# Cross-covariance attention and a squared-ReLU expert on one core: transposed scores, k's norms by ones matmuls, inverse norms on ScalarE, another order of the first loads

## The chip, the cores and the metric

The kernel runs on one core of a Trainium2 chip. The time is device microseconds of one launch, the median of several executions. The notes on the chip that are drawn on are called the Trainium skill, by page title and section.

## The reference

```python
B, N, C = (4, 6080, 256); d_ff = 2048; tau = 1.0
qn = q / (np.linalg.norm(q, axis=1, keepdims=True) + 1e-06)   # norms over the tokens
kn = k / (np.linalg.norm(k, axis=1, keepdims=True) + 1e-06)
s = kn.transpose(0, 2, 1) @ qn / tau                          # 256 x 256 per batch
a = softmax(s, axis=-1)
x = (v @ a).reshape(B * N, C)
h = x @ w_in                                                  # 24320 x 2048
r = np.maximum(h, 0.0)
g = moe_s * (r * r) + moe_b
out = g @ w_out
```

Per batch there is a small reduction (scores and norms over 6080 tokens, a 256 x 256 softmax) and then a large expert, whose matmuls fill TensorE. The kernel folds the attention into the expert's weights: `wa = a @ w_in`, so that `h = v @ wa`.

## The kernel before

It walks over 48 groups of 512 tokens, each in 16 steps. A step `m` makes one 128-row tile of `h` for a group (`mm1`), plus seven of the 112 small matmuls of a seven-product scheme for the group before. Every second step ends with a relu on ScalarE. The reduction of the *next* batch is threaded through the same steps: loads, score matmuls, squares, and near the end of the batch a list of finishing operations, each put at a step by a table called `FIN` (number 0 falls in step 8 of a group, 3 in step 11, 8 in step 0 of the next group).

All operations are recorded in program order on each engine, so an engine that must wait holds up everything behind it. In what follows, a *finish* is the whole list of finishing operations of one batch, an *expert pair* is the two matmuls of `mm1` in a step, a *fold* is an operation that makes 256 or 512 columns of `wa`, and PSUM is the memory into which the matmuls write their results.

```python
# products: X, Z, Y are halves of PSUM tiles; a tile is one bank
def begin(name):
    t = ps_o.tile([P, 2, 2 * P], FP32, tag="o_ps", name="o_ps")
    halves = [t[:, h, :].rearrange("p (j c) -> p j c", j=2) for h in range(2)]
    if name == "X":
        st["X"] = halves[0]
        x_tile[0] = t              # its second half serves the norms
    else:
        st["Z"], st["Y"] = halves
# order of the seven products: X Z X Y X Z X, 16 matmuls each, from step 3 on

# ... scores of one piece of tokens, s = k^T q
nc.tensor.matmul(self.s_ps[:, ch, :], kc[:np_, j, ts(ch, P)], qc[:np_, j, :], ...)

# ... add_norms, later batches: 8 matmuls of one column, 4 sums of squares for k and 4 for q
self.n_all = x_tile[0][:, 1, : 2 * CH].rearrange("p (a c) -> p a c", a=2)
nc.tensor.matmul(self.n_ps[a][:, ch : ch + 1], t[:np_, a, j, ts(ch, P)], ones16[:np_, 0:1], ...)

# ... finishing, later batches: FIN = (0, 3, 5, 7, 15, 17, 19, 22)
norms:   add_norms, then sqrt on ScalarE as Ln and Exp(0.5 x)       # k and q together, 4 columns
recip:   add EPS and reciprocal on VectorE
split:   s * 1/|k| in two fp16 halves (VectorE), each through DMA transposes
join:    sum of the two transposed halves (VectorE)
exps(j): eT = Exp(1/|q| * sT)  on ScalarE, one half each            # 1/|q| is a per-partition scale
sums:    row sums of eT by 4 one-column matmuls, reciprocal on VectorE
folds:   wa = eT^T @ w_in, scaled by 1/row sum on the way out of PSUM
```

For batch 0 there is no earlier batch to hide behind. Its finish stands alone in front: transposes by TensorE in fp32, the first eight 256-column folds, then the main loop.

## Time and profile before

| | before |
|---|---|
| time, median of 3 | 718.86 us (718.62 to 719.0) |
| profiled span | 717.2 us |
| first expert matmul | 38.60 us |
| TensorE's recorded waits from 60 to 700 us | 0.2 us |

How to read it: TensorE is the bound from the first expert matmul on, so what counts is each pause of TensorE after that, and when that matmul starts.

### The profile page before, as it was taken

Reading aid. Unit: us, or ns where it says so; the run is one execution under the profiler, and the core shown is the slowest. Engines: PE = TensorE matmul, PEld = TensorE weight load, DVE = VectorE, ACT = ScalarE, POOL = GpSimd, SP = SyncE. Lnnn points to the kernel's source line nnn. Section 1 sums busy time; section 2 is a strip of 40 time slices with the busy share of each in tenths; the row PEclk is TensorE's granted clock in tenths of the full one; section 3 lists DMA queues with packets and bytes.
Section 4 is the critical chain, followed back from the end, with each engine's and each line's share of the span. In section 5 each row is a group of like instructions: output and inputs, shape, how many; then the busy total and the mean of one; then the engine's idle time right before and its main releaser. Section 6 shows DMA issues by size and latency. Waiting matters only on the chain.

```text
span 717.2 us, 17629 instructions
## 1 busy us (share of the span) xinstructions
PE 698.9 (97%) x7479; PEld 504.6 (70%) x7479; DVE 626.1 (87%) x882; ACT 536.5 (75%) x579; POOL 109.8 (15%) x189
## 2 busy tenths in 40 slices
PE   4799999999999999999999999999999999999998
PEld 2556777776677777777677777777668777777777
DVE  4879999999789999999889899999887888888886
ACT  4479877787777777777777778777877777777875
POOL 4532332101201222111110222110000000000000
PEclk9999999999999999999999999999999999999999
DMA  9999998647556879443972877944423333321201
GB/s 236 207 259 172 159 170 137 111 108 129 119 107 114 144 133 145 108 93 83 154 151 57 141 138 124 154 90 86 105 63 75 93 71 74 97 60 46 83 30 74
DMA packets 89790, 84.25 MB, mean 117 GB/s; under 512 B 59664, under 2 KB 64848, under 8 KB 89712
## 3 DMA queue, kind: packets, MB, share of 16 engines
q0 software_dynamic: 26064, 43.40, 37.5%
q1 hardware_dynamic: 63072, 38.43, 21.5%
q8 instruction: 58, 0.95, 0.6%
q10 hardware_dynamic: 576, 1.31, 0.5%
q14 instruction: 20, 0.16, 0.1%
HBM read 78.91 MB, written 24.90 MB: 145 GB/s over the span
## 4 chain that ended last, share of the span: by engine, by line
PE 93%; DMA 4%; DVE 1%; ACT 1%; POOL 1%; issue 0%; POOLq 0%; ACTq 0%
PE h_ps L641 45%; PE o_ps L809 40%; PE s_ps L146 4%; DMA qk<-in_q_dram 3%; PE wa_ps L326 2%; DMA v<-in_v_dram 1%; PE o_ps L713 1%; PE o_ps L687 0%; POOL qk L130 0%; ACT r L651 0%; DVE o_sb L669 0%; DVE S L737 0%; DVE sq L166 0%; DVE S L735 0%; DVE S L739 0%
## 5 line engine op out<-in xcount | busy, mean ns | idle before, releaser
L651 ACT ACTIVATE r<-h_ps 128x1024 f16<-128x1024 f32 (+1 forms) x384 | 388.4, 1014 | 153.4 <-PE h_ps L641 150.9
L641 PE MATMUL h_ps<-vT,wa 128*128 128x512 f16 (+7 forms) x1632 | 452.1, 364 | 0.1
L809 PEld LDWEIGHTS <-S 128*128 128x128 f16 x2944 | 198.0, 98 | 85.0 <-issue 0.9
L809 PEld LDWEIGHTS <-g 128*128 128x128 f16 x2208 | 155.0, 98 | 74.1
L664 DVE TENSOR_TENSOR g<-r 128x2048 f16<-128x2048 f16 (+2 forms) x150 | 174.8, 1165 | 14.6 <-ACT r L651 14.5
L809 PE MATMUL o_ps<-T,S 128*128 128x128 f16 x2208 | 183.3, 219 | 0.1
L641 PEld LDWEIGHTS <-wa 128*128 128x128 f16 x1632 | 135.9, 98 | 20.6 <-ACT wa L319 0.3
L809 PE MATMUL o_ps<-w_out,g 128*128 128x128 f16 x1472 | 134.2, 219 | 0.2 <-DVE u L669 0.2
L669 DVE SCALAR_TENSOR_TENSOR o_sb<-o_ps,s_out,u 128x256 f32<-128x256 f32 x138 | 66.5, 482 | 47.1 <-PE o_ps L809 44.5
L662 ACT ACTIVATE g<-r 128x1024 f16<-128x1024 f16 (+1 forms) x97 | 100.4, 1035 | 0.2
L146 PE MATMUL s_ps<-qk 128*128 128x256 f16 (+1 forms) x384 | 69.6, 281 | 14.0 <-ACT qk L137 8.7
L379 POOL DMA_DIRECT2D v<-in_v_dram x48 | 31.3, 656 | 263.5 <-DMA vT<-v 209.6
L669 DVE SCALAR_TENSOR_TENSOR u<-o_ps,s_out,rowconst 128x256 f32<-128x256 f32 x138 | 66.0, 478 | 0.0
L809 PE MATMUL o_ps<-w_out,S 128*128 128x128 f16 x736 | 63.5, 219 | 0.0
L809 PE MATMUL o_ps<-N,g 128*128 128x128 f16 x736 | 63.4, 219 | 0.0
L193 POOL DMA_DIRECT2D f<-f x30 | 26.3, 877 | 225.6 <-DVE f L182 172.0
L169 ACT ACTIVATE sq<-qk 128x1024 f16<-128x1024 f16 (+3 forms) x49 | 50.4, 1033 | 10.0 <-DMA qk<-in_k_dram 6.7
L737 DVE TENSOR_TENSOR S<-S,g 128x2048 f16<-128x2048 f16 (+1 forms) x47 | 56.4, 1201 | 1.3
L735 DVE TENSOR_TENSOR S<-g 128x2048 f16<-128x2048 f16 (+1 forms) x47 | 56.1, 1193 | 0.0
L741 DVE TENSOR_TENSOR S<-g,S 128x2048 f16<-128x2048 f16 x46 | 56.0, 1217 | 0.0
L739 DVE TENSOR_TENSOR S<-g 128x2048 f16<-128x2048 f16 x46 | 55.9, 1216 | 0.0
L146 PEld LDWEIGHTS <-qk 128*128 128x128 f16 (+1 forms) x384 | 32.8, 101 | 20.1 <-DVE qk L136 8.0
(74 smaller groups left out, 314.9 us busy)
## 6 DMA issues: line engine op xcount, KB each, us to landing
out_dram<-o_sb SPq DMA_DIRECT2D x46, 512.0 KB, 3.0
v<-in_v_dram POOLq DMA_DIRECT2D x47, 256.0 KB, 4.7
qk<-in_k_dram POOLq DMA_DIRECT2D x42, 256.0 KB, 6.1
qk<-in_q_dram POOLq DMA_DIRECT2D x42, 256.0 KB, 7.2
f<-f POOLq DMA_DIRECT2D x30, 128.0 KB, 3.1
vT<-v SPq DMA_TRANSPOSE x182, 3.2
w<-in_moe_w_out_dram POOLq DMA_DIRECT2D x4, 512.0 KB, 11.3
raw<-in_k_dram SPq DMA_DIRECT2D x2, 512.0 KB, 6.4
```

Of the source, the lines that this page charges most:

```text
L146: po(nc.tensor.matmul(self.s_ps[:, ch, :], kc[:np_, j, ts(ch, P)], qc[:np_, j, :], start=(c == 0 and j == 0 and ch == 0), stop=(c == len(s ...
L169: po(nc.scalar.activation(out=st["sq"][:np_, 1, js, :], in_=kc[:np_, js, :], func=AF.Square))
L641: po(nc.tensor.matmul(dst, wa[:, ci, ts(m, P)], src, start=(ci == 0), stop=(ci == CH - 1), skip_group_check=True))
L651: po(nc.scalar.activation(out=r16[:, :, i % 2, :n], in_=h_tiles.pop((g, i))[:, :, :n], func=AF.Relu))
L662: po(nc.scalar.activation(out=dst, in_=src, func=AF.Square))
L664: po(nc.vector.tensor_mul(dst, src, src))
L669: po(nc.vector.scalar_tensor_tensor(out=dst, in0=src, scalar=s_out, op0=ALU.mult, in1=add, op1=ALU.add))
L735: po(nc.vector.tensor_add(T[1], A21, A22))
L737: po(nc.vector.tensor_sub(T[2], T[1], A11))
L739: po(nc.vector.tensor_sub(T[3], A11, A21))
L741: po(nc.vector.tensor_sub(T[4], A12, T[2]))
L809: po(nc.tensor.matmul(st[name][:, j, :], a()[:, i, ts(j, P)], w[:, i, :], start=first, stop=last, skip_group_check=True))
```

## The change

Its intent: with `sT = q^T k` computed directly, nothing has to be transposed. The inverse norm of k then lies along the free axis and must be equal in all partitions; a matmul with a 128 x 128 matrix of ones gives it so, as a row of 256 columns. The inverse norms become four dependent activations on ScalarE (logarithm, root, logarithm of root + EPS, exp of its negative), and VectorE has one product left. In front, the last k rows are loaded ahead of the last q rows, and v ahead of w_in, so that k's path is done when q arrives.

```diff
-                    kc[:np_, j, ts(ch, P)],
-                    qc[:np_, j, :],
+                    qc[:np_, j, ts(ch, P)],
+                    kc[:np_, j, :],
 ...
+                if a == 1:
+                    po(nc.tensor.matmul(self.n_ps[1], ones16[:np_, :], t[:np_, 1, j, :],
+                                        start=start, stop=end, skip_group_check=True))
+                    continue
 ...   (root, recip, split, join and turn are removed)
+            def inverse(a):
+                n = (CH, C)[a]
+                r = sm_pool.tile([P, n], FP32, tag=f"r{a}", name=f"r{a}")
+                act(self.n_ps[a], AF.Ln, bias=tiny)
+                act(r, AF.Exp, scale=0.5)
+                act(r, AF.Ln, bias=eps)
+                act(r, AF.Exp, scale=-1.0)
+            def scale(halves=1):
+                    po(nc.vector.tensor_mul(st["t"][:, js], self.s_ps[:, js],
+                                            rk[:, None, :].broadcast_to((P, n, C))))
 ...
+            front = [norms(1), lambda: inverse(1), norms(0), lambda: inverse(0),
+                     lambda: scale(CH if self.b == 0 else 1)]
             return front + [lambda: exps(0), lambda: exps(1), sums] + folds
 ...   (first batch: NLATE = 3 late pieces, all k parts before all q parts; fewer filler matmuls)
-    load_w_in(0, NW)
     load_v(0)
+    load_w_in(0, 2 * P)
+    load_w_in(2 * P, NW)
 ...   (first batch: one fold ahead of the main loop, in place of three)
-    for f in fin[6:12]:
+    for f in (exps0, exps1, row_sums, folds[0]):
 ...
-    FIN = (0, 3, 5, 7, 15, 17, 19, 22)
+    FIN = (0, 3, 16, 18, 20, 21, 22, 24)
-    FOLDS = (0, 0, 3, 4, 7, 8)
+    FOLDS = (0, 0, 1, 1, 3, 4, 7, 8)
```

## The prediction

> **What bounds the kernel now.** I read the page's busy line first, then the table of stretches, then the chain, then timelines of the two places that the change touches.
>
> ```profile
> PE 698.9 (97%) x7479; PEld 504.6 (70%) x7479; DVE 626.1 (87%) x882; ACT 536.5 (75%) x579; POOL 109.8 (15%) x189
> ```
>
> TensorE says 97% busy, but its ends are modelled, so I checked it by stretches (columns: stretch, length, then busy time of PE, PEld, DVE, ACT, POOL, the granted clock, DMA share, GB/s).
>
> ```profile
> 0.00:36.50 36.50, 21.85 (x183) 14.65 (x183) 23.12 (x47) 16.94 (x21) 18.97 (x39) 1.00 1.06 221
> 38.60:51.90 13.30, 13.30 (x78) 7.26 (x79) 9.92 (x17) 10.85 (x13) 3.72 (x7) 1.00 1.08 276
> 51.90:73.60 21.70, 21.34 (x164) 14.09 (x163) 21.08 (x37) 20.62 (x26) 5.31 (x10) 1.00 1.07 177
> 73.60:710.00 636.40, 636.38 (x6991) 463.78 (x6990) 568.44 (x776) 485.84 (x517) 80.62 (x131) 1.00 0.55 106
> ```
>
> All of TensorE's idle time lies before 36.5 us, where the loads of batch 0's q and k run at a DMA share above 1. After 73.6 it misses 0.02 us in 636. To be sure that this is real work, I added up the matmuls of a stretch as columns at 2.4 GHz plus 2.4 ns each: 13.20 us of work in 38.6 to 51.9 (13.3 long), 21.14 in 51.9 to 73.6 (21.7 long). So from the first expert matmul at 38.60 on, TensorE is the bound and only its instruction count and its stalls matter. The chain shows what sets 38.60 (start, length, what):
>
> ```profile
> 18.76 9.74 DMA qk<-in_q_dram
> 28.78 7.72 DMA v<-in_v_dram
> 36.55 0.62 PE vT_ps L390 x8
> 37.68 0.90 PE wa_ps L326 x8
> 38.60 0.60 PE h_ps L641 x2
> ```
>
> The first v tile lands last and TensorE's in-order queue puts its transposes ahead of the row sums. Yet v is hardly alone there. The timeline of the front (start, length, engine, line, operation) has a second path of the same length:
>
> ```profile
> 33.94 1.04 PE L146 MATMUL s_ps<-qk 128*128 128x256 f16 x8
> 35.44 0.26 ACT L235 ACTIVATE nrm<-n_ps,tiny 128x2 f32<-128x2 f32 x1 [1.47 <-PE n_ps L224]
> 36.43 0.84 ACT L299 ACTIVATE eT<-t_ps,rnrm 128x256 f16<-128x256 f32 x2 [0.50 <-PE t_ps L293]
> 37.44 0.24 PE L309 MATMUL r_ps<-parts,eT 128*128 128x1 f16 x4
> 37.54 1.03 PE L326 MATMUL wa_ps<-w_in,eT 128*128 128x256 f16 x8
> ```
>
> The exponentials end at 37.27 and the row sums start 0.17 later, a normal handover. Removing v alone would therefore win about nothing.
>
> **What the Trainium skill says.** "ScalarE: Activation LUTs", What ACT_TABLE_LOAD costs: an ACTIVATE with a pointer bias takes about 280 ns + 0.833 ns per column, an immediate one 186 ns + 0.833, and neighbours overlap by about 93 ns. The trace agrees: 0.26 and 0.20 us for two columns, 0.47 to 0.50 for 256 columns (the exponentials), 1.02 for 1024 columns that start 0.92 apart. "TensorE: Matmul & The Clock Gate", Wait — 56ns, not 53.3ns?: N columns take N/2.4 GHz plus 2.5 ns; the trace has two 512-column matmuls per 0.43 us. Same page, What's actually happening: the array falls to half clock after an idle window of about 3.4 us; the granted clock is 1.00 in every stretch here, and no run so far shows a drop. "VectorE: DVE Perf Modes", The TRN2 errata: an fp32 tensor_tensor takes (N+151)/0.96 ns, 691 for 512; the trace has 684.
>
> **Front, part by part.** *Removed:* the four fp32 transposes (0.74 us, 35.64 to 36.38) and the add and reciprocal of each norm. *Moved:* the last three k pieces come ahead of the last q's. A 256 KB piece takes 1.25 us (issues of a k and q pair are 2.5 us apart), so k is complete about 1.25 us earlier, near 31. v moves ahead of 256 KB of w_in: 36.5 becomes about 35.3. The last q does not move: the score matmuls of the last two pieces ran back to back from 33.94, so it landed by about 34.3.
>
> *k's path.* TensorE has 10 ones matmuls of 256 columns (1.1 us, the tenth after the fold that ends near 30.5), 20 one-column ones for q (0.033 each, 0.65), then 8 of 256 (0.86): about 32.3. Then ScalarE does four dependent activations of 256 columns, (0.47 + 0.44 + 0.50 + 0.44) plus about 0.03 between: 1.95 us, to about 34.4. It ends just before q's does, so it is hidden.
>
> *q's path.* Last q 34.2, square 0.4, sums and handover: Ln near 35.05 (35.44 before). Four small activations of 0.29, 0.23, 0.29, 0.23 end near 36.1; the scaling by VectorE (two of about 0.45 from 34.9) ends first. Exponentials at 36.15 in place of 36.43, so the first expert matmul at about 38.3, a gain of 0.3 us.
>
> *Given back.* Before, TensorE did eight 256-column w_in folds between the row sums and 38.60, while it would have waited for the scaling anyway. Now it does four there and four after the first expert matmuls: 4 x 0.109 = 0.43 us moved from a wait into the bound stretch. The front nets 0.1 us slower (from 0.5 faster to 0.4 slower).
>
> **Later batches, three times.** *Removed:* about 2.6 us of VectorE (0.16 + 0.18 + 0.68 + 0.87 + 0.69) for one product of 0.69, and four small DMA transposes. VectorE and DMA bound nothing there, so: 0. *TensorE:* 8 one-column matmuls (0.26) become 2 of 256 and 4 of one column (0.21 + 0.13): +0.08 us. *ScalarE:* two small activations become four of 256 columns back to back, then four small ones half a group later. Here is ScalarE at the old place:
>
> ```profile
> 146.30 1.03 ACT L651 ACTIVATE r<-h_ps 128x1024 f16<-128x1024 f32 x1
> 147.27 0.26 ACT L235 ACTIVATE nrm<-o_ps,tiny 128x4 f32<-128x4 f32 x1
> 147.56 0.20 ACT L236 ACTIVATE nrm<-nrm 128x4 f32<-128x4 f32 x1
> 147.72 1.02 ACT L651 ACTIVATE r<-h_ps 128x1024 f16<-128x1024 f32 x1
> 149.42 1.02 ACT L651 ACTIVATE r<-h_ps 128x1024 f16<-128x1024 f32 x1 [0.68 <-PE h_ps L641]
> 151.07 1.02 ACT L651 ACTIVATE r<-h_ps 128x1024 f16<-128x1024 f32 x1 [0.62 <-PE h_ps L641]
> ```
>
> The relus come every 1.645 us. The order of instructions puts the new four between two relus: 0.97 + 0.50 + 0.47 + 0.53 + 0.34 = 2.81 us from relu to relu, so the second is 1.17 late. There are two h buffers. A buffer's next writer starts three groups of items (0.39 each) and two pairs (0.43) after its pair ends, 2.03 us; the relu needs 0.17 + 1.02 + 0.1. Slack 0.74, stall 0.43. A lateness already in the trace says it is a little worse: two squares between the relus at 113.12 and 115.93 made it 0.94 late at a longer beat of 1.865, and the six relus after them came 0.2 to 0.3 late in sum where this model gives about 0. So 0.43 to 0.65. The four small ones (1.05 us, 0.3 late) fit; the two exponentials now sit together behind VectorE's product and may be 0.7 late, costing 0 to 0.1. Per batch 0.5 to 0.8, taken as 0.65: +1.9 us for three.
>
> Sum: 718.9 + 0.1 + 1.9 = 720.9. I take 720.3, since a hand-placed schedule may have room that I don't see.
>
> **Rivals.** (1) The front wins about 1 us and ScalarE's bursts are absorbed. For it: the transposes leave a path that really ends the front, and in the stretch from 51.9 to 73.6 ScalarE (20.62 of 21.7) and VectorE (21.08) leave TensorE 0.56 us short, so relus that start earlier might recover some. Against: the last q is fixed by DMA, and the 0.43 us of folds. Time: 717.7. (2) k's inverse norms become the front's wait: if its sums come later than 32.3, ScalarE, in order, starts q's logarithm late, microsecond for microsecond. For it: ScalarE and TensorE have only some 0.5 us in hand. Time: up to 722.5. (3) With fewer filler matmuls TensorE falls to half clock near 36 us. Against: its gaps stay below 1.5 us. It would cost 2 us: 722.5.
>
> **Range and chances.** Front from 0.9 faster to 1 slower, the batches from 0 to 2.7: 717.6 to 722.4 holds 8 in 10. 2% is 14.4 us; all of TensorE's idle time is about 18, nearly all under loads whose bytes do not change. Faster 0.005, slower 0.01.
>
> **What would show it.** First expert matmul between 37.9 and 38.6, v's transposes earlier by a microsecond and no longer in the chain, four w_in folds behind it. In each later batch four activations in a row, the next relu about 1.2 us late, and TensorE idle or a longer beat of 0.4 to 0.7 us just there and nowhere else. I am wrong if the relu's lateness leaves TensorE's beat unchanged, if the first expert matmul comes before 37.5, or if the stretch to 73.6 shrinks by more than 0.5 us.

## More of the kernel before

The later batches are finished in three places. The table of stretches around them has the stretch, its length, the busy time of TensorE, of its weight loads, of VectorE, ScalarE and GpSimd, the granted clock, the DMA share and GB/s:

```profile
140.90:176.00 35.10, 35.10 (x386) 24.70 (x384) 32.30 (x46) 28.24 (x33) 3.18 (x6) 1.00 0.55 114
313.00:348.00 35.00, 35.00 (x384) 24.55 (x382) 32.04 (x45) 27.91 (x33) 3.17 (x6) 1.00 0.54 109
486.00:524.00 38.00, 38.00 (x416) 26.77 (x415) 34.79 (x49) 29.95 (x34) 1.58 (x3) 1.00 0.39 90
```

Length and TensorE's busy time agree to the last digit: the old finish cost no pause that this view shows. The ends of matmuls are modelled, so a short pause can hide in it: at the old logarithm the small matmuls follow the expert pair after 0.49 us (147.09 to 147.58), elsewhere after 0.43. Two places of the timeline of TensorE in the first of them will matter (start, length, engine, line, operation, output and inputs, shape, count):

```profile
150.04 0.22 PE L809 MATMUL o_ps<-w_out,g 128*128 128x128 f16 x1
150.10 0.50 PE L809 MATMUL o_ps<-T,S 128*128 128x128 f16 x6
...
165.34 0.24 PE L309 MATMUL r_ps<-parts,eT 128*128 128x1 f16 x4
165.45 0.59 PE L641 MATMUL h_ps<-vT,wa 128*128 128x512 f16 x2
```

At 150.10 product 4 takes over tile X from product 3 in tile Y, without a gap. At 165.34 the four row sums pass in 0.11 us.

## The result

The changed kernel took 723.85 us (median of 5, 723.39 to 725.03), the kernel before 719.00 in the same rounds (718.62 to 719.84). The ratio is 1.0070, with a 95% interval of 1.0058 to 1.0082. The ratios are made from the runs of both kernels, and not quite the ratios of the two medians. At the 2% bar this is the same time; against the interval it is plainly slower, by almost 5 us, and it lies outside the predicted range of 717.6 to 722.4.

The profiled span is 721.9 us against 717.2. The three finishing stretches of the changed kernel, columns as above:

```profile
140.90:176.00 35.10, 34.34 (x374) 24.12 (x372) 30.08 (x40) 28.77 (x38) 3.17 (x6) 1.00 0.53 114
313.00:348.00 35.00, 34.24 (x379) 24.29 (x377) 29.68 (x40) 28.12 (x37) 3.72 (x7) 1.00 0.46 91
486.00:524.00 38.00, 37.24 (x406) 26.23 (x404) 32.52 (x45) 31.06 (x39) 1.60 (x3) 1.00 0.35 83
```

TensorE misses 0.76 us in each, where it missed nothing. VectorE is less busy by 2.2 to 2.4 us in each, as intended, and that is worth nothing. The waits of TensorE from 60 to 700 us name the cause (engine, output, line, what it waited for: us in total, times, longest):

```profile
PE o_ps L786 <- ACT r L247: 1.8, 3, 0.6
PE r_ps L280 <- ACT eT L270: 0.5, 3, 0.2
```

L247 is the logarithm of k's norm sums. The timelines of ScalarE and TensorE there:

```profile
150.14 1.02 ACT L628 ACTIVATE r<-h_ps 128x1024 f16<-128x1024 f32 x1 [0.56 <-PE h_ps L618]
151.06 0.47 ACT L247 ACTIVATE r<-o_ps,tiny 128x256 f32<-128x256 f32 x1
...
152.87 1.00 ACT L628 ACTIVATE r<-h_ps 128x1024 f16<-128x1024 f32 x1
```

```profile
150.76 0.22 PE L786 MATMUL o_ps<-w_out,g 128*128 128x128 f16 x1
151.58 0.49 PE L786 MATMUL o_ps<-T,S 128*128 128x128 f16 x6 [0.60 <-ACT r L247]
```

This is the handover from product 3 to product 4 of the fence before: 0.06 us apart there, 0.82 here. The logarithm reads the norm sums in the second half of tile X; product 4 writes the first half of the same tile, and starts only when the logarithm has ended at 151.53. The relu behind the four activations is indeed late (2.73 us after the last one), but no wait of TensorE for a relu is listed.

The second wait is where the row sums are made. The timeline of all three engines there:

```profile
167.05 0.68 DVE L264 TENSOR_TENSOR sm_t<-s_ps,r 128x512 f32<-128x512 f32 x1
167.83 0.91 ACT L270 ACTIVATE eT<-sm_t,r 128x256 f16<-128x256 f32 x2 [1.00 <-DVE sm_t L264]
168.46 0.17 PE L280 MATMUL r_ps<-parts,eT 128*128 128x1 f16 x1
168.79 0.23 PE L280 MATMUL r_ps<-parts,eT 128*128 128x1 f16 x3 [0.16 <-ACT eT L270]
168.88 0.59 PE L618 MATMUL h_ps<-vT,wa 128*128 128x512 f16 x2
```

ScalarE stands still for 1.00 us until VectorE has made the product, the exponentials come late, and from the first row sum to the next expert matmul TensorE now needs 0.42 us instead of 0.11: 0.31 more.

In front the first expert matmul is where it was (38.62 against 38.60). The lines that answer to those in the prediction:

```profile
35.51 0.26 ACT L247 ACTIVATE r<-n_ps,tiny 128x2 f32<-128x2 f32 x1 [0.65 <-PE n_ps L234]
36.60 0.91 ACT L270 ACTIVATE eT<-sm_t,r 128x256 f16<-128x256 f32 x2
38.62 0.60 PE L618 MATMUL h_ps<-vT,wa 128*128 128x512 f16 x2 [0.37 <-ACT wa L290]
```

From q's logarithm to the first exponential it is 1.09 us now and was 0.99 (35.44 to 36.43): the chain of four activations is no shorter than two, two small VectorE operations and four transposes beside them.

To place the loss in time, I took the start of each relu in both profiles and subtracted. The lateness is 0.76 us from the fourth relu up to the first later batch's finish, then grows by 1.03, 1.14 and 1.14 us in the three finishes and by nothing anywhere else, to 4.06 at the last relu. The span differs by 4.7. The remaining 0.65 lies after the last VectorE operation, which ends 2.72 us before the end of the span before (714.00 + 0.48, of 717.2) and 3.37 us after the change. The last VectorE operation, and the DMA view of the window from 718 us to the end:

```profile
718.05 0.48 DVE L670 SCALAR_TENSOR_TENSOR o_sb<-o_ps,s_out,rowconst 128x256 f32<-128x256 f32 x1 [1.26 <-PE o_ps L664]
```

```profile
q14 instruction: 1, 0.01, 0.5%
```

An instruction fetch lies in the last half microsecond. The same window of the kernel before has none.

### The profile page after: what moved, and what is told of

It reads as the page before. A ratio compares the mean times of both kernels' runs of the same rounds, so it can differ in the third digit from the quotient of the medians.

```text
span 721.9 us, 17552 instructions
## 1 busy us (share of the span) xinstructions
PE 699.9 (97%) x7458; PEld 504.8 (70%) x7458; DVE 620.2 (86%) x864; ACT 542.8 (75%) x599; POOL 110.2 (15%) x188
## 4 chain that ended last, share of the span: by engine, by line
PE 87%; ACT 4%; DMA 4%; DVE 2%; issue 1%; POOL 0%; POOLq 0%; ACTq 0%; DVEq 0%
PE h_ps L618 42%; PE o_ps L786 37%; PE s_ps L148 4%; DMA qk<-in_k_dram 3%; ACT r L628 2%; PE wa_ps L297 2%; DMA qk<-in_q_dram 1%; ACT g L639 1%; ACT r L247 1%; PE o_ps L690 1%; DVE g L641 1%; ACT eT L270 1%; PE o_ps L664 0%; DVE u L646 0%; POOL qk L132 0%
## 5 line engine op out<-in xcount | busy, mean ns | idle before, releaser
L177 ACT ACTIVATE sq<-qk 128x1024 f16<-128x1024 f16 (+1 forms) x47 | 49.2, 1050 | 8.7 <-DVE f L190 4.4
```

The source lines that it names most:

```text
L177: po(nc.scalar.activation(out=st["sq"][:np_, 1, js, :], in_=kc[:np_, js, :], func=AF.Square))
```

## The experiments

Seventeen kernels were run besides the changed one, all of them correct. "Lateness" is that of the relus against the profile of the kernel before: after the front (the seventh relu) and at the last relu. "Idle" is TensorE's missing time in the three finishing stretches together. A pause of some 0.15 us can hide in "idle", since the ends of matmuls are modelled; the lateness has no such gap. "Tail" is from the end of the last VectorE operation to the end of the span, good to 0.05 us, since the span is printed to 0.1. Rows without a ratio were single looks.

| kernel | time, us | before, us | ratio (95%) | front | idle | last relu | tail |
|---|---|---|---|---|---|---|---|
| changed kernel | 723.85 | 719.00 | 1.0070 (1.0058–1.0082) | 0.76 | 2.28 | 4.06 | 3.37 |
| e1_ln_early | 723.14 | 719.73 | 1.0052 (1.0037–1.0067) | 0.43 | 1.41 | 3.36 | 3.36 |
| e2_ln_late_spread | 723.86 | 719.73 | 1.0061 (1.0044–1.0078) | 0.99 | 2.29 | 4.30 | 3.33 |
| e3_ln_early_rest_later | 722.45 | 719.73 | 1.0043 (1.0028–1.0058) | 0.97 | 0.90 | 2.88 | 3.35 |
| e4_sums_later | 723.97 | 719.73 | 1.0063 (1.0048–1.0078) | 0.86 | 2.55 | 4.44 | 3.29 |
| e5_folds_before | 723.12 | 719.54 | 1.0050 (1.0033–1.0066) | 0.28 | 2.34 | 3.68 | 3.35 |
| e7_before_v_first | 719.10 | 719.54 | 0.9995 (0.9980–1.0010) | 0.32 | 0 | 0.24 | 2.68 |
| e8_spread_scale_early | 721.68 | 719.54 | 1.0031 (1.0014–1.0048) | 1.00 | 0.39 | 2.16 | 3.38 |
| e9_spread_and_folds | 721.00 | 719.54 | 1.0022 (1.0007–1.0037) | 0.33 | 0.39 | 1.47 | 3.36 |
| e10_norms_step6 | 722.15 | 719.16 | 1.0038 (1.0023–1.0053) | 0.16 | 1.14 | 2.56 | 3.37 |
| e11_ln_step10 | 723.90 | 719.16 | 1.0065 (1.0048–1.0082) | 1.06 | 2.04 | 4.12 | 3.31 |
| e13_twelve_sp | 723.19 | 719.16 | – | 0.92 | 2.31 | 4.28 | 2.65 |
| e14_eighteen_dve | 723.99 | 719.16 | – | 1.05 | 2.32 | 4.42 | 3.30 |
| e15_front_only | 719.77 | 719.12 | 1.0006 (0.9994–1.0019) | 0.54 | 0 | 0.42 | 2.61 |
| e16_front_only_mended | 718.65 | 719.12 | 0.9993 (0.9979–1.0006) | -0.14 | 0 | -0.26 | 2.69 |
| e12_all_mended | 719.93 | 719.12 | 1.0011 (0.9998–1.0023) | -0.18 | 0.39 | 0.96 | 2.67 |
| e17_front_two_steps | 718.46 | 719.19 | 0.9990 (0.9976–1.0003) | -0.34 | 0 | -0.46 | 2.69 |
| e18_eight_sp | 723.43 | 720.09 | – | 0.86 | 2.34 | 4.22 | 3.00 |

One caution for the column "front": ten profiles here have the changed kernel's front unchanged (the changed kernel, e1, e2, e3, e4, e8, e11, e13, e14, e18; e15 would be an eleventh), and they show 0.43 to 1.06. Differences under 0.3 us in it cannot be read from a single profile. The growth in the finishes repeats to 0.1.

### Which wait: e1, e2, e3, e4

Theory A: TensorE waits for the first logarithm's read of tile X. Theory B, the prediction's: the burst of four activations makes a relu late and TensorE waits for an `h` buffer.

**e1_ln_early** moves the burst of four to the step of the norm sums:

```diff
-    FIN = (0, 3, 16, 18, 20, 21, 22, 24)
+    FIN = (0, 0, 16, 18, 20, 21, 22, 24)
```

> Edit to the changed kernel: in batches 1 to 3 the four activations of k's inverse norms follow right behind the ones matmuls (same step) in place of three steps later. Theory A (TensorE's next product into tile X waits 0.65 us until the first logarithm has read the norms that lie in the same tile): that wait disappears from the waits list, each batch loses 0.65 us of its 1.1, total about -1.9 us against the changed kernel (near 722). Theory B (my prediction: the relu behind the four activations comes too late and TensorE waits for an h buffer): the burst now follows two squares and makes a relu about 1.6 us late, so TensorE stalls 0.4 to 0.9 us there and nothing is won, or it gets worse (723.8 or more).

The wait for L247 went. In its place stood a smaller one, for the relu:

```profile
PE h_ps L618 <- ACT r L628: 0.5, 3, 0.2
```

The idle time fell from 2.28 to 1.41 us, but the lateness grew by 2.93 us over the three finishes, where the changed kernel's grew by 3.30; of the 0.70 us by which its last relu leads the changed kernel's, 0.33 lie in the front, which varies. So only about 0.1 us per finish was won, not 0.65. Both theories are partly right: where the logarithm stops being a listed wait, the late relu becomes one, and 0.23 us stay at the logarithm in a form that the list of waits does not show (see e9).

**e2_ln_late_spread** leaves the logarithm where the change has it, and sets the other three activations apart:

```diff
             front = [norms(1), lambda: inverse(1), ...
+                front[1:2] = [lambda i=i: inverse_part(i) for i in range(4)]   # later batches
-    FIN = (0, 3, 16, 18, 20, 21, 22, 24)
+    FIN = (0, 3, 5, 7, 9, 16, 18, 20, 21, 22, 24)
```

> Edit to the changed kernel: the first logarithm stays three steps behind the ones matmuls, the other three activations of k's inverse are spread two steps apart each, so no relu is more than about 0.3 us late. Theory A: TensorE's wait of 0.6 us for the logarithm stays, total unchanged (723.5 to 724). Theory B: the stall disappears with the burst, 0.65 us per batch, total near 722.

The wait for the logarithm stayed whole, 1.8 us in three times, and so did the time. The lateness grew by 3.31 us, as in the changed kernel. Without any burst the loss is the same, so in the changed kernel the burst is not what is paid for.

**e3_ln_early_rest_later** is the reverse, the logarithm alone in step 8 and the other three as a burst in step 11 (`FIN = (0, 0, 3, 3, 3, 16, ...)`).

> Edit to the changed kernel: the first logarithm right behind the ones matmuls, the other three activations as a burst three steps later. Theory A: as the early run, the wait goes, total near 722 (-1.9). Theory B: three activations make the relu about 0.8 us late in place of 1.2, so most of the stall goes as well, near 722. This run does not separate the two; it is there to be the best placement of both.

Neither wait is left there, and the idle time falls to 0.90 us, most of it the row sums. The first part of a batch's loss, as lateness, went from 0.72 to about 0.25.

**e4_sums_later** moves only the row sums, three steps later (`FIN[7] = 27`).

> Edit to the changed kernel: the row sums and the w_in folds behind them come three steps later in batches 1 to 3. If the second part of a batch's loss (0.32 to 0.42 us) is TensorE waiting in order for the second exponential, it goes: -1.0 to -1.2 us in all (near 722.7), and the row sums' wait for the exponentials is left in the front only. If it is due to the relus behind the exponentials being late, nothing changes (723.8).

The wait for the exponentials went from the later batches, and this came for it:

```profile
PE h_ps L618 <- ACT r L628: 0.7, 3, 0.3
```

The exponentials themselves are late and hold the next relu, so moving their reader only moves the wait. Time and idle did not fall.

### Tile X again: e10, e11

**e11_ln_step10** changes one number of the changed kernel: the burst comes one step earlier, `FIN[1] = 2`.

> The changed kernel with one number changed: the burst of four activations on k's norms one step earlier (step 10 for step 11), so that the first logarithm runs while TensorE is in product 3 (tile Y), and ends ahead of product 4, the next into X. Theory A (the wait is for the logarithm's read of tile X): TensorE's wait for L247 (1.8 us in 3 times) is gone. The burst (1.9 us) now stands ahead of the relu of step 11, so that relu is late by more and theory B of the prediction (h buffer) shows: a wait of TensorE for the relu of 0.2 to 0.6 per batch. Batch costs 0.6 to 1.0, last relu 2.6 to 3.8 late, time 722.5 to 723.5. If instead any chain of four activations costs the same wherever it stands, the time stays at 723.8 and the wait for L247 stays.

```profile
PE h_ps L618 <- ACT r L628: 1.5, 3, 0.5
```

The wait for the logarithm is gone and the prediction's kind of wait stands there instead, listed as 0.5 us each and 0.67 in lateness. The time did not change; that is dearer than I had expected (last relu 4.12 us late, not 2.6 to 3.8). The burst stands elsewhere here, and the relu behind it starts 3.03 us after the one before (148.86 and 151.89), not 2.81. The prediction's model, fed with that, gives 3.03 - 1.645 - 0.74 = 0.65, so its slack is right. It does not follow that the changed kernel would show 0.43 once the logarithm's wait were gone: no run has the burst at its place without that wait. So far as shown, two waits of similar size lie close together, and the prediction computed the one that did not come first.

**e10_norms_step6** takes e9 (below) and makes k's norm sums and their logarithm two steps earlier, in step 6, while TensorE works on tile Z (`FIN = (-2, -2, 3, 5, 7, 16, 18, 9, 21, 23, 26)`).

> As e9 (single activations spread over steps, scaling at its old place, folds ahead of the main loop), but k's norm sums and their first logarithm two steps earlier, in step 6, while TensorE writes product 1 into the Z tile; the next product into X starts some 1.2 us later. Theory A (TensorE waits because product X and the norms share a PSUM tile, so what counts is whether X is being written while the logarithm reads): the 0.17 us that e9 still shows per batch at the logarithm goes; each later batch costs 0.15 to 0.25 us against before instead of 0.31 to 0.42, the last relu stands 1.0 us after before's instead of 1.47, time 720.3 to 720.7 with before at 719.5. Rival B (the residual is the extra activations on ScalarE, wherever they stand): 0.3 to 0.4 per batch stays, time as e9, 721.0.

My expectation failed, and it was dearer instead of cheaper. TensorE's timeline in the first finish:

```profile
145.01 0.55 PE L796 MATMUL o_ps<-T,S 128*128 128x128 f16 x7
145.67 0.38 PE L230 MATMUL o_ps<-f,ones 128*128 128x256 f16 x2
...
146.99 0.33 PE L796 MATMUL o_ps<-T,S 128*128 128x128 f16 x3 [0.28 <-ACT r L264]
```

The norm sums start 0.66 us after the seven small matmuls ahead of them began; elsewhere the next matmul follows such a seven after 0.39 us. VectorE reads the first product out of tile X from 145.14 to 145.62 just there, so I take the sums' start at 145.67 for the end of that read; the profile does not name the wait. Then the logarithm stands behind a square on ScalarE until 146.46, and product 2, the next into X, waits for it. The tile is shared by three engines, and a free window of it must be free for all three.

### Spreading and the folds: e5, e8, e9

**e5_folds_before** makes the first three folds ahead of the main loop, as before the change.

```diff
-    for f in (exps0, exps1, row_sums, folds[0]):
+    for f in (exps0, exps1, row_sums, *folds[:3]):
-    FOLDS = (0, 0, 1, 1, 3, 4, 7, 8)
+    FOLDS = (0, 0, 3, 4, 7, 8)
```

> Edit to the changed kernel: batch 0's four w_in folds of columns 256 to 511 go back ahead of the first expert matmul, into the wait for the scaling, and the other folds get their old steps. Theory: the front's loss of 0.76 us (4 x 0.109 = 0.43 us of folds moved behind the first expert matmul, and 0.33 us in which the fifth expert pair waits for VectorE's scaling of a fold that now queues behind a square) goes: relus 3 to 56 come 0.0 to 0.2 us after the old kernel's in place of 0.76 (the last q's landing varies by some 0.3 us), total near 723.0. Rival: the loss sits in the later first row sums; then the relus stay 0.7 or more behind.

The front's lateness is 0.28; in e9 and e10, which have the same front, it is 0.33 and 0.16. The mean of the three is 0.26, that of the ten unmended fronts 0.89. The moved folds thus cost about 0.6 us: 0.43 of TensorE's work (4 x 0.109) and the rest a wait for VectorE, which scales the second fold behind a square that itself waits for a relu.

**e8_spread_scale_early** separates all four activations, with the logarithm in the step of the sums, puts VectorE's product back to the place of the old scaling, and moves exponentials and sums behind it (`FIN = (0, 0, 3, 5, 7, 16, 18, 9, 21, 23, 26)`; the eighth number is the product). **e9_spread_and_folds** is e8 with e5's front.

> Edit to the changed kernel, batches 1 to 3: first logarithm right behind the ones matmuls, the other three activations two steps apart each, VectorE's product nine steps after the matmuls in place of twenty, so that the exponentials don't wait for it, the exponentials two steps apart, row sums three steps later. Theory: all of a batch's loss but the 0.08 us of extra matmul columns goes, 1.0 us per batch: relus at the end 1.0 to 1.3 us behind the old kernel's (front 0.8 and 3 x 0.1) in place of 4.06; total near 720.8. If something else in the later batches costs, more than 0.3 us per batch stays.

> The last edit together with the folds put back: relus at the end 0.2 to 0.5 us behind the old kernel's, total 719.0 to 719.8, the same as before. If the losses do not add up, it stays above 720.5.

In e8 and e9 only 0.13 us of idle time per finish is left, and no wait for L247, a relu or the exponentials is listed in the finishes. Both expectations were missed: e8 came at 721.68 us, and e9 at 721.00, above the 720.5 from which the losses were said not to add up. The tail's 0.65 us was not in the sum, and each finish still costs 0.31 to 0.42 us in place of 0.1. TensorE's timeline of e9 shows where:

```profile
147.44 0.59 PE L628 MATMUL h_ps<-vT,wa 128*128 128x512 f16 x2
148.16 0.49 PE L796 MATMUL o_ps<-T,S 128*128 128x128 f16 x6
```

The small matmuls, which go on writing tile X, start 0.72 us after the expert pair, not 0.43; the logarithm reads the same tile from 147.64 to 148.11. Only 0.13 us of this pause is shown as idle. All three finishes have it, in e1, e3, e8, e9 and e12 alike (0.72 each); the kernel before, whose logarithm has 4 columns and takes 0.26 us, has 0.49. So 0.23 us per finish is tile X again. With the estimate of 0.08 for the wider norm sums, 0 to 0.1 us per finish is left that no view shows as a wait.

### The loads: e7

**e7_before_v_first** is the kernel *before* with one line moved, `load_v(0)` ahead of `load_w_in(0, NW)`.

> Edit to the kernel before: only the first v load goes ahead of the first w_in load. The chain of the kernel before names v as the last to land. My reading: the exponentials' path is as long, so the time stays (first expert matmul within 0.2 us of 38.6, total within 0.5 us of before). Rival: v bounds, and the first expert matmul comes 0.5 us or more earlier.

```profile
PE r_ps L309 <- ACT eT L299: 0.2, 1, 0.2
```

v is no longer waited for, the exponentials are, and the first expert matmul came at 38.92, no earlier than 38.60 (and 0.3 us later, where 0.2 was expected at most). The time is the same (ratio 0.9995). That agrees with the prediction's reading that v was one of two equal paths.

### The tail: e13, e14, e18

**e13_twelve_sp** and **e18_eight_sp** add tiny copies (4 bytes, SBUF to SBUF) on SyncE's queue to the changed kernel, twelve and eight, and **e14_eighteen_dve** adds eighteen tiny memsets on VectorE.

```diff
+        for i in range(4):                       # e13; in e18: eight, in batch 2 only
+            at_step(w1 - fin_len + 2 * i, lambda i=i: po(nc.sync.dma_start(
+                out=spare[:, i : i + 1], in_=ones32[0:1, i : i + 1])))
```

> On the last 0.66 us: in every run of the changed form the span ends 3.3 us after VectorE's last operation starts to be done, in the kernel before 2.7, and only there an instruction fetch (queue 14, one packet of 8 KB) lies in the last half microsecond. The changed kernel with twelve tiny copies more on SyncE's queue (four per later batch), so that SyncE issues as many DMAs as before. Theory T1 (the fetch, or the order of the last waits, is SyncE's and follows from its count of instructions): the fetch at the end goes and the end is 2.7 us after VectorE's last operation. Theory T2 (it is another engine's): the fetch stays at the end and the tail stays 3.3. Time else as the changed kernel, 723.8.

> The changed kernel with eighteen tiny memsets more on VectorE (six per later batch), so that VectorE has as many operations as before. If the instruction fetch at the end is VectorE's, it moves off the end and the tail shrinks from 3.3 to 2.7 us; if it is SyncE's or ScalarE's, the tail stays 3.3. The memsets cost some 0.06 us each on an engine that is not the bound: time 723.8, less 0.6 if the tail goes.

> The changed kernel with eight tiny copies more on SyncE's queue, all in batch 2's finish. Theory F (an instruction fetch that falls at the very end): the count of SyncE's instructions moves on by eight, so the fetch comes some groups earlier, no packet of queue 14 lies after the last store, and the tail from the end of VectorE's last operation is 2.6 to 2.7 us. Theory L (the order in which the end of the program waits for the stores' semaphores): the last stores have the same semaphores as in the changed kernel, so the tail stays 3.3 us. Time else as the changed kernel, 723.2 or 723.8.

With twelve copies the fetch left the end and the tail shrank to 2.65 us (the last packet of queue 14 starts at 721.5 us in the changed kernel, at 716.7 with eight copies, at 695.9 with twelve: it moves with SyncE's count); with the memsets it stayed at 3.30 with the fetch. Over all profiles the tail takes two values: 2.61 to 2.72 in the seven whose SyncE issues as many DMAs as before the change, 3.29 to 3.38 in the eleven with twelve fewer. e18 lies between, at 3.00: no fetch is left at the end, but the last stores have the semaphores of the changed kernel. The waits of SyncE at the end of e18:

```profile
SPq L877 <- DMA out_dram<-o_sb: 3.5, 4, 1.6
```

The changed kernel has the same 3.5 us in four waits, the kernel before and e13 have 3.2 in three. So of the 0.65 us about 0.35 goes with the fetch and the other 0.3 with how the stores are waited for, each from one profile; the second is read from these lists and was not changed by itself. Neither of e18's two theories was right alone. The change has twelve DMA transposes fewer on SyncE, and this is a side effect of their number, not of what they did.

### Front and later batches apart: e15, e16, e12, e17

**e15_front_only** has the changed front and loads, and the kernel before in batches 1 to 3.

```diff
-    grams = {b: Gram(b, chunks_first if b == 0 else chunks_later) for b in range(B)}
+    grams = {b: Gram(b, chunks_first) if b == 0 else GramLater(b, chunks_later) for b in range(B)}
-    FIN = (0, 3, 16, 18, 20, 21, 22, 24)
+    FIN = (0, 3, 5, 7, 15, 17, 19, 22)          # GramLater is the class of the kernel before
```

> The change undone in the later batches: the first batch and all loads as in the changed kernel, batches 1 to 3 exactly as in the kernel before (k's sums as columns, scaling split in two halves, DMA transposes). Theory A (the later batches alone cost the 3.3 us, the front 0.4 to 1.0, the tail's 0.66 follows SyncE's count of instructions, which here is before's again): the last relu stands 0.4 to 1.0 us after before's, the same distance as right after the front; no wait of TensorE for L247; the tail is 2.7 us; time 0.4 to 1.1 us over before, ratio 1.0006 to 1.0015. Rival (the changed front moves the loads and so disturbs the later batches too): 2 us or more are left.

The finishing stretches are full again:

```profile
140.90:176.00 35.10, 35.10 (x386) 24.65 (x384) 32.39 (x46) 27.80 (x32) 3.18 (x6) 1.00 0.56 111
```

The lateness stays what the front gave it, the tail is 2.61, and the time is within 0.1% of before. The later batches alone make the 3.3 us.

**e16_front_only_mended** adds to it e5's folds, two activations for an inverse norm, and q's last products ahead of q's last norm sums. **e17_front_two_steps** is e16 without the last of these.

```diff
-                act(r, AF.Exp, scale=0.5)
-                act(r, AF.Ln, bias=eps)
-                act(r, AF.Exp, scale=-1.0)
+                act(r, AF.Exp, scale=-0.5)     # EPS = 1e-6 is left out
```

> As e15, with three changes in the front: the first three folds ahead of the main loop as in before; the inverse norm in two activations, exp(-0.5 ln(sum)), which leaves EPS out (1e-6 beside norms of some 55: below the output's precision); q's last products ahead of q's last norm sums. Theory (after q's last sums the path is the chain of four activations, then the exponentials, so two activations fewer, 0.29 + 0.20 us and their gaps, are gained whole, and some 0.1 from the order of sums): first expert matmul at 37.9 to 38.1 instead of 38.62, last relu 0.4 to 0.7 us ahead of before's; time 718.8 to 719.2 with before at 719.5, ratio 0.9990 to 0.9996. Rival (VectorE's product or v's transposes end last there): 0.2 us or less gained, ratio 1.0 or more.

> e16 without the new order of q's sums: changed front with two activations for an inverse norm and three folds ahead of the main loop, later batches as before. If the path after q's last sums is the chain of activations, the time from the first logarithm of q's norms to the first exponential is 0.5 us instead of 1.09, and q's last norm sums end 0.2 to 0.4 us after q's last product starts instead of 0.9, so the first expert matmul comes 0.2 to 0.5 us earlier than e16's 38.45, if q's last pieces land no later; last relu 0.4 to 0.7 us ahead of before's, ratio 0.9985 to 0.9993. If VectorE's product now ends last (it needs the same last matmul as the sums), the first exponential waits for it and only 0 to 0.2 us are gained on e16.

EPS = 1e-6 is left out beside norms of some 7.8 (0.1 times the root of 6080; the expectation of e16 names 55, which is wrong and changes nothing), and both kernels are correct. The two activations fewer are gained in the chain. From q's logarithm to the first exponential it takes 0.53 us in both, instead of 1.09:

```profile
35.68 0.26 ACT L247 ACTIVATE r<-n_ps,tiny 128x2 f32<-128x2 f32 x1 [1.51 <-PE n_ps L234]
36.21 0.91 ACT L268 ACTIVATE eT<-sm_t,r 128x256 f16<-128x256 f32 x2
```

The first expert matmul came at 38.45 in e16 and 38.23 in e17, against 38.76 to 38.91 in e5, e9 and e10, which have the same three folds ahead of it. For e16 37.9 to 38.1 and a lead of 0.4 to 0.7 us at the last relu had been expected; it got 38.45 and 0.26. The new order of sums in e16 put all 16 of them (0.54 us) behind q's last product; it won nothing, and part of the difference may be q's landing. e17 is 0.46 us ahead of the kernel before at the last relu, and 718.46 against 719.19 us in time. Its interval, 0.9976 to 1.0003, just includes 1, so it is the best version here but not shown to be faster.

**e12_all_mended** keeps the change in all batches, with every remedy: spreading, folds, two activations, the copies on SyncE's queue.

> The changed kernel in all batches with every remedy: folds ahead of the main loop, k's logarithm in the step of its sums, the second activation alone four steps later, scaling at its old place, exponentials at steps 21 and 23 of the finish, two activations for an inverse norm, q's products ahead of its sums, and twelve tiny copies on SyncE's queue as in e13. If the causes add up: e9's last relu offset of 1.47, less 0.6 in the front, so 0.7 to 1.0 us; tail 2.7; time 0.6 to 1.1 us over before, ratio 1.0008 to 1.0016. If they don't, more than 1.5 us remain, ratio above 1.002.

It came at 719.93 us, inside the expectation, so the causes found by then add up. It is still 0.96 us late at the last relu: its front is 0.18 ahead, and its three finishes cost 1.1 us.

## Why the prediction was wrong

It gave 720.3 us with a range up to 722.4, and the time was 723.85. The main view was right: TensorE is the bound from the first expert matmul on, the savings on VectorE and DMA are worth nothing, v was not alone in front, the clock stays full, and each later batch loses time where k's norms are read (though in a second place as well). By its steps:

- **k's path in front: held.** Its four activations ran from 32.95 to 34.86, hidden, predicted 32.3 to 34.4. None of the rivals happened: the front won nothing and the bursts cost (1), q's logarithm waited 0.65 us for its own sums, not for k's activations (2), and the clock stayed at 1.00 (3).
- **q's path: mis-sized by 0.3.** "Ln near 35.05" was 35.51, so the first expert matmul came at 38.62 and not 38.3. TensorE waited for q's last pieces (0.25 us at 34.22), and their products and norm sums then came one after the other. In e15 the same front gave 35.28 and 38.40, so about half of this is how the loads fall.
- **Folds moved into the bound stretch: held in kind, mis-sized.** 0.43 us was right for the work; the wait for VectorE's scaling between relus was not foreseen. e5, e9 and e10 put the whole at about 0.6. With the first expert matmul 0.3 late the front made 0.76 instead of 0.1.
- **"Slack 0.74, stall 0.43": the wrong wait.** The step took the relu's lateness (2.81 us from relu to relu predicted, 2.73 seen) and from it a wait for the `h` buffer. But the logarithm had moved from the step of the sums, where it took 0.26 us and cost 0.06, to three steps later, exactly where product 4 takes over X. TensorE's wait for it, listed as 0.60 us and 0.76 from start to start (0.82 against 0.06), came first and left the relu's lateness nothing to cost. e2 shows that the wait is the logarithm's and not the burst's, e3 that it goes when the logarithm moves away, e11 that the wait for the `h` buffer exists and that its slack was rightly worked out. That the 0.65 taken for a batch comes near to what this wait cost was luck.
- **"Costing 0 to 0.1" for the exponentials behind VectorE's product: mis-sized.** The row sums took 0.31 us longer in the first later batch, and the second part of a finish cost 0.31 to 0.42.
- **Per batch**: 0.65 predicted; 1.03 to 1.14 measured, from these two terms (0.72 and 0.31 to 0.42). Three times the difference is about 1.3 us.
- **The tail**: 0.65 us that had no step at all. e13, e14 and e18 tie it to the number of DMAs on SyncE's queue.
- **The shading**: the sum was 720.9, and 0.6 us were taken off for room in the schedule that I had not seen. The runs show none; what was hidden was another wait.

The terms: 718.9 + 0.76 + 3.3 + 0.65 = 723.6, against 723.85. What stays open: why q's last pieces land as they do, and 0 to 0.1 us per finish in e9 and e12.

Three readings of the prediction do not hold as they stand, though the error above does not come from them. Not all of TensorE's idle time lies before 36.5 us: 14.65 of its 18.3 us do, and 3.2 lie after 710 us, in the tail that then grew. The 21.14 us of work from 51.9 to 73.6 are nearer 20.5, since the two fp32 matmuls there start 0.22 us apart, so that stretch is about 1.2 us short and not 0.56. And the 684 ns set beside the 691 belong to an operation that reads PSUM and writes fp16; the one such fp32 sum of 512 columns within SBUF took 690.

On the shared tile the Trainium skill agrees: "PSUM — Partial Sum Buffer", PSUM bank collisions raise a hardware error, says that two engines must be kept from one bank and quadrant of PSUM at once even when they touch different columns, and asks for semaphores by bank and quadrant, or simply by bank, not by address. The program guards its tile, which is one bank, in this way. The trace shows the price of it: a matmul into columns 0 to 255 stood until the read of columns 256 to 511 was over (151.53, then 151.58). Reading that section against the two halves of tile X would have pointed to the right wait.

On the tail: "Runtime: NRT & Kernel Launch", Instruction fetch mechanics, says that instructions are fetched in blocks by DMA while earlier ones run, so that the fetch is normally hidden, and that a taken branch outside the window stalls. The trace agrees for the run as a whole (the 16 KB fetches, 58 of them, leave no gap in TensorE's stretches before), and differs at the end, where the one fetch went with about 0.35 us.

## What to carry to other kernels

When an operation is moved along a full schedule, look up who else uses the tile that it reads, not only the tile that it writes: a bank that holds two things makes the readers of one wait for the writers of the other, and the place was free at the old step by luck or by design. When two waits could follow from one move, work out both and take the one that comes first; removing it will show the second. An engine with spare time on average can still cost the bound engine time, if what it does last stands in front of something due.

## What the Trainium skill lacked or had wrong

- "Runtime: NRT & Kernel Launch", Instruction fetch mechanics: it gives 16 KiB blocks and no other size. The trace has 16 KB packets on one queue of instructions (58 packets, 0.95 MB) and 8 KB ones on another (20 packets, 0.16 MB). It also has no figure for a fetch that falls on the end of a program; here it went with about 0.35 us, gone in e18 when eight copies were added.
- No page says that the end of a program can take longer by how the last stores' semaphores are waited for: 3.5 us in four waits against 3.2 in three, about 0.3 us of the span (read from the lists of waits, not tested by itself).
- "ScalarE: Activation LUTs", What ACT_TABLE_LOAD costs: neighbouring activations overlap by about 93 ns. That holds for the relus here (1.02 us long, 0.92 apart), but not for activations that each read the one before: 0.47 us long, the next starts 0.50 us after it (33.26 and 33.76 in e17). A chain should be summed without the overlap and with 0.03 us between.
- "PSUM — Partial Sum Buffer", PSUM bank collisions raise a hardware error: it has the rule but no cost. Here guarding by bank cost TensorE 0.60 us of listed wait each time that product 4 met a read of the other half, and 0.23 us where the logarithm had been moved back to the step of its sums.
